# DeltaNet attention with an FNet block: loads 6 and 7 in program order on all engines, the second weight matrix ahead of the third inversion, GpSimd's arithmetic on VectorE, unread products ahead of load 0

## The chip, the cores and the metric

The kernel runs on one core of a Trainium2 chip. The time is the device time of one execution in microseconds (us); the figure for a kernel is the median of its runs. A profiled execution also has a span, from its first to its last instruction, and the mean clock that TensorE was granted (1.0 is full speed). The engines are called as the profile calls them: PE (TensorE, matmul; PEld is its loading of weights), DVE (VectorE), ACT (ScalarE), POOL (GpSimd) and SP (SyncE, which here only issues DMAs).

## What is computed

Attention of the "delta" kind, for B = 4 batches, H = 8 heads, S = 768 steps and heads of D = 48, then a block that mixes with Fourier transforms:

```python
k_n = k / (norm(k, axis=-1) + 1e-6)
for t in range(S):                       # one 48 x 48 state for each batch and head
    y[t]  = q[t] @ state
    state = state + beta[t] * outer(k_n[t], v[t] - k_n[t] @ state)
x  = y as (B, 768, 384)
u  = x + real(fft(fft(x, axis=1), axis=2))
un = (u - mean(u)) / sqrt(var(u) + 1e-6)
out = u + relu(un @ w_ch1) @ w_ch2       # w_ch1 384 x 1536, w_ch2 1536 x 384
```

All arrays are float32 but the two weight matrices, which arrive as float64 and are converted on the chip.

## The kernel before, in words

**Loads, rounds, batches.** The sequence is cut into 24 *loads*, g = 0 to 23: 128 steps of all 8 heads of one batch, 6 loads (`NL`) for a batch. A load has two chunks of 64 steps. Within a chunk the recurrence is solved with the inverse of a unit lower triangular matrix; between chunks the state goes on. Four loads (`RL`) make a *round*: their 32 triangular matrices are inverted together, all on DVE. Rounds 0 to 2 invert blocks of 16 (`invert16`, L451; the first transpose is L468, the row-by-row pairs are L510 and L513, the last transposes L516 and L518), rounds 3 to 5 blocks of 32 (`invert`, L392; transpose L398, pairs L439 and L443, last transposes L446 and L447). So the third inversion is `invert16(2)` and the fourth `invert(3)`. The matrix M that each fills is set to zero first, on POOL. In the four loads of the next round, the inverse is what everything else hangs on.

**The parts of a load.**
- *Keys* (`pre_a`, L316): the key rows are turned by four 128x128 transposes on PE (`turn`, L308; PE line L113), ACT copies them out as KT (L314), PE forms the products of keys with keys, and the triangular part goes to G and GU. In `gram16` (L351) ACT and DVE fill G (L372, L376, L378), and GU is made by DVE in one masked product for the first four loads (L383), by ACT in three small copies for the others (L388).
- *Queries* (`pre_q`, L524): the same turn gives QT; then products of keys and queries, masked by DVE into LQ (L548).
- *After the inversion* (`pre_m16`, L591, for rounds up to 2; `pre_m`, L551, later): the blocks of the inverse are put together to MT with ACT copies (Z L601, MT L617 and L640) and PE products, and V is scaled (L622 on DVE for loads under 8; on POOL otherwise, there and at L562). In batch 0 U0 and WT are made in addition.
- *Recurrence* (`step`, L671): `S,KT` products on PE, V minus these on DVE (L691), `V,MT` products, U copied out by ACT (L701), `U,K` products, and the new S on DVE (L730, L732).
- *Outputs* (`outputs`, L735): `S,QT` products into one PSUM pair, copied to x by ACT (L755), `U,LQ` products, added to x by DVE (L765). Chunk 0 of a batch's first load has no state, so its half of the pair is set to zero by DVE (L745) ahead of the products.

**After a batch's six loads** come `folds` (L772: sums and differences of rows and columns, L786 to L804; the two E of rows, L786 and L788, on POOL from batch 1 on, except in the last tile), `fourier` (L809: products with tables, x L873 to L876, statistics, the reciprocal root on POOL) and `mlp` (L889: un on DVE, turned by PE (`ptr`) and copied by ACT (L911, unT), the products `ph` with the first matrix, ReLU on ACT (L921, hT), the products `po` with the second matrix, the add to x L932, and the store). `mlp` of one batch is cut into pieces that are woven into the loads of the next batch.

**The weights** (`weights`, L221) are converted in 24 pieces of 384x128 or 128x384, 12 for each matrix. A piece arrives as two 32-bit words for each number. ACT converts the low word (L277) and a clamp (L272); DVE picks bits with five instructions (L278, L282, L283, L292, L294); POOL multiplies the two parts (L287), into w1 or w2; then SP issues the load of a later piece into the slot of the ring that came free. The ring has 4 slots for w1 and 3 for w2. Each `yield` is half a piece. The variable `conv` is this generator.

**What sets the order.** The parts are Python generators, and `advance` runs one of them to its next `yield`. Under `tc.manual_schedule(engines=...)` the named engines keep the order in which the program issues; the others are ordered by the framework's scheduler. Batch 0 is written out by hand, under PE, DVE, ACT and POOL. From load 6 on, `period(g, side)` (L991) does one load in six slots: the two chunks of the recurrence, the outputs, the next load's `pre_q` and `pre_m`, the keys and the inversion of the next round at so many yields for each slot, the folds, and `side`, the `mlp` of the batch before, up to a quota `want`. Loads 6 and 7 run under PE alone, loads 8 to 23 under all four:

```python
        inv = invert16(2)
    with tc.manual_schedule(engines={mybir.EngineType.PE}):
        drain(nq)
        for g in range(NL, NL + 2):
            period(g, side)
    with tc.manual_schedule(engines=engines):
```

DMAs are issued from SP, in program order unless the scheduler orders them, and a few from POOL and ACT at the start.

**Unread products.** Ahead of load 0's recurrence PE runs five products of 128x384 that nobody reads (`spin(5)`, L1122; the product is L1119), of `ident`, a part of the constant `pack`, with zeros. They come just before the first use of the first inverse.

All products pass one helper line each: L110 for products, L113 for transposes.

Of the kernel before, what the change touches and what calls it, by code (L numbers as in the profile page):

```python
# [20 lines left out]
RL = 4  # L21
RING = 7
V16 = 16
R16 = 3
# [40 lines left out]
def kernel(  # L65
# [126 lines left out]

    early = w2.rearrange("p c m -> p (c m)").rearrange("p (n h d) -> p n h d", h=8, d=64)
    nc.vector.memset(early[:, :, :, D:64], 0.0)
    early = [early[:, i] for i in range(9)]
# [25 lines left out]
    def weights():  # L221
# [13 lines left out]
        for last, pieces in enumerate(sets):  # L235
# [33 lines left out]
            for i in range(len(pieces) + 1):  # L269
                if i > 0:  # L270
                    lo0, hi0, man0, num0 = of(i - 1)
                    nc.scalar.activation(num0, num0, ACT.Relu, bias=low_e)  # L272
                if i < len(pieces):
                    lo, hi, man, num = of(i)


                    nc.scalar.activation(man, lo.bitcast(U32), ACT.Copy, scale=2.0 ** -52, bias=1.0)  # L277
                    nc.vector.tensor_scalar(num, hi, 0xFFFFF, None, op0=ALU.bitwise_and)  # L278
                yield
                if i > 0:  # L280

                    nc.vector.tensor_scalar(num0, num0, 255, 2.0 ** 23, op0=ALU.min, op1=ALU.mult)  # L282
                    nc.vector.scalar_tensor_tensor(num0, hi0, -2 ** 31, num0, op0=ALU.bitwise_and,  # L283
                                                   op1=ALU.bitwise_or)
                    dst = pieces[i - 1][1]
                    c = dst.shape[1]
                    nc.gpsimd.tensor_tensor(dst, man0.rearrange("p (c f) -> p c f", c=c),  # L287
                                            num0.bitcast(F32).rearrange("p (c f) -> p c f", c=c),
                                            op=ALU.mult)
                    stage(i - 1 + deep)  # L290
                if i < len(pieces):
                    nc.vector.scalar_tensor_tensor(man, num, 2.0 ** -20, man, op0=ALU.mult,  # L292
                                                   op1=ALU.add)
                    nc.vector.tensor_scalar(num, hi, 20, 0x7FF, op0=ALU.logical_shift_right,  # L294
                                            op1=ALU.bitwise_and)
                yield
# [54 lines left out]
    def gram16(g, KT, G):  # L351
# [3 lines left out]
        if g == 0:  # L355
            GXs["O"] = wk.tile([128, RL, 8, C], F32, tag="O", name="GU4")
        if first:
            GU = GXs["O"][:, g]
        else:
            GU = wk.tile([128, 8, C], F32, tag="GX", bufs=4, name="GU")  # L360
            nc.gpsimd.memset(GU[:, :, 0:V16], 0.0)
        GXs[g, 16] = GU
# [10 lines left out]
        for hh in range(2):  # L373
# [3 lines left out]
            else:  # L377
                nc.scalar.activation(dst[rw], src[rw, :, :, W:C], ACT.Copy)  # L378
        if g == 2 * RL - 1:
            yield  # L380
        dst = GU.rearrange("p (i a) s -> p a i s", a=2)
        if first:
            nc.vector.tensor_tensor(dst, src, m_up[:, None, None, :].broadcast_to([128, 2, 4, C]),  # L383
                                    op=ALU.mult)
        else:
            for e in range(1, 4):
                cs = slice(V16 * e, V16 * e + V16)
                nc.scalar.activation(dst[:, :, :, cs], src[:, :, :, cs], ACT.Copy,  # L388
                                     scale=m_ahead[:, e - 1:e])
        yield  # L390

    def invert(r):  # L392
# [3 lines left out]
        M = wk.tile([128, W, W], F32, tag="M", name="M")  # L396
        nc.gpsimd.memset(M, 0.0)
        nc.vector.transpose(A, G.rearrange("p m s -> p s m"))  # L398
# [52 lines left out]
    def invert16(r):  # L451
# [14 lines left out]
        A, M, Ad, Md = whole(A2), whole(M2), blocks(A2), blocks(M2)  # L466
        nc.gpsimd.memset(M2, 0.0)
        nc.vector.transpose(A, G.rearrange("p m s -> p s m"))  # L468
# [82 lines left out]
    def pre_m(g):  # L551
# [9 lines left out]
                                op=ALU.mult)  # L561
        nc.gpsimd.tensor_tensor(V.rearrange("p c j d -> p (c j) d"),  # L562
                                V.rearrange("p c j d -> p (c j) d"),
# [27 lines left out]
    def pre_m16(g):  # L591
# [28 lines left out]
        def scaled_v():  # L620
            V = Vs.pop(g)
            (nc.vector if g < 2 * RL else nc.gpsimd).tensor_tensor(  # L622
                V.rearrange("p c j d -> p (c j) d"), V.rearrange("p c j d -> p (c j) d"),
                nT[:, m8, None].broadcast_to([128, 8, D]), op=ALU.mult)
            return V
# [109 lines left out]
    def outputs(g):  # L735
# [7 lines left out]
        pq = ps_pair()  # L743
        if n == 0:
            nc.vector.memset(pq[full[0], :, 0:4 * D], 0.0)  # L745
        for j in range(2):
            for hh in range(2):
                for cc in range(2):
                    for jp in range(2):
                        if n == 0 and cc == 0:  # L750
# [3 lines left out]
                           S[(b, 2 * n + cc)][lo[jp], hh, j, :], j == 0 and hh == 0)  # L754
        nc.scalar.activation(x.rearrange("p (i a e) -> p a i e", a=2, e=D),  # L755
                             pq[:, :, 0:4 * D].rearrange("p a (i e) -> p a i e", e=D), ACT.Copy)
        yield
# [6 lines left out]
        xv = x.rearrange("p (h e) -> p h e", h=2)  # L764
        nc.vector.tensor_tensor(xv, xv, pl[:, :, 0:4 * D], op=ALU.add)  # L765
        yield
# [5 lines left out]
    def folds(b):  # L772
# [11 lines left out]
        for t in range(TH):  # L784
            eng = nc.gpsimd if b and t < TH - 1 else nc.vector
            eng.tensor_tensor(E[:, 0, t], x[:, t], x[:, TH + t], op=ALU.add)  # L786
            yield
            eng.tensor_tensor(E[:, 1, t], x[:, t], x[:, TH + t], op=ALU.subtract)  # L788
            yield
# [198 lines left out]
    done = 0  # L988
    pm = inv = late = None

    def period(g, side):  # L991


        nonlocal pm, inv, late, done, fold
        b, n = divmod(g, NL)
# [19 lines left out]
        if more:  # L1015
# [7 lines left out]
            elif g + 1 >= 2 * RL:  # L1023
                pm = pre_m16(g + 1)
                if not fresh:
                    behind[0].append(pm)
                for i in range(4):
                    pieces[i + (2 if fresh else 1)].append(pm)
        if not last_round and r > 1:
            if li == 0:  # L1030
                load_beta(r + 1)
            keys = {0: ((0, 1), (2, 3), (4, 5)), 1: ((0, 1),)}.get(li, ())
            for i, (s0, s1) in enumerate(keys):
                k4 = pre_a(RL * (r + 1) + 3 * li + i)
                behind[s0].append(k4)
                pieces[s1].append(k4)
        for i in range(SLOTS):
            if i == (2 if r + 1 < R16 else 3) and fresh and inv:
                drain(inv)
# [3 lines left out]
            if i == 5 and n + 1 == NL:  # L1043
                o = outputs(g)
                drain(o)
                late = None
            if li == 1 and i == 1 and r > 1 and not last_round:
                inv = invert(r + 1)
            if g == NL:
                advance(inv, 4)  # L1050
                advance(conv, 3)
            elif inv:
                advance(inv, 8 if r + 1 < R16 else 6)
            if n + 2 >= NL and 0 < i < 5:
# [7 lines left out]
            else:  # L1062

                want = 2 + KF + (2 + 2 * KF) * at // (2 * SLOTS)
                if n > 1:
                    want = 4 + 3 * KF + (PIECES - KEEP - 4 - 3 * KF) * (at - 2 * SLOTS) // (
                        SLOTS * (NL - 2))
            for p in behind[i]:
                advance(p)
            advance(side, want - done)  # L1070
            done = max(want, done)
        load_v(g + 2)

    engines = {mybir.EngineType.PE, mybir.EngineType.DVE, mybir.EngineType.Activation,
               mybir.EngineType.Pool}
    with tc.manual_schedule(engines=engines):
# [5 lines left out]
        ms = [pre_m16(g) for g in range(2 * RL)]  # L1082
        for g in range(RL):
            advance(keys[g])
            if g > 0:
                drain(keys[g - 1])
        drain(keys[RL - 1])
        advance(inv0, 2)
        for g in range(3):
# [21 lines left out]
        advance(keys[-1])  # L1111
        idle = wk.tile([128, DM], F32, tag="un", bufs=2, name="idle")
        nc.gpsimd.memset(idle, 0.0)
        unread = ps_post([128, 512], "unread")

        def spin(n):

            for _ in range(n):
                nc.tensor.matmul(unread[:, 0:DM], lhsT=ident, rhs=idle, start=True, stop=True,  # L1119
                                 skip_group_check=True)  # L1120

        spin(5)  # L1122

        advance(ms[0], 2)
        advance(qs[1])
# [10 lines left out]
        advance(inv1, 5)  # L1136
        drain(keys[-1])
        first = part(conv, 2 * KF + 2)
# [125 lines left out]
        for fc in range(KF):  # L1264
            if converted < 2 * KF + 2:
                convert(2)
            else:
                advance(conv)
            advance(side)
            if fc % 3 == 1:  # L1270
                advance(f)
# [8 lines left out]
        inv = invert16(2)  # L1280
    with tc.manual_schedule(engines={mybir.EngineType.PE}):
        drain(nq)
        for g in range(NL, NL + 2):
            period(g, side)
    with tc.manual_schedule(engines=engines):
        for b in range(1, B):
            for g in range(max(NL * b, NL + 2), NL * (b + 1)):
                period(g, side)
# [44 lines left out]
```

## Time and profile before

| | |
|---|---|
| runs | 762.54, 759.20 and 761.86 us, median 761.86 |
| the profiled execution's own time | 760.74 us |
| its span | 759.0 us |
| its mean granted clock | 0.973 |
| PE busy | 691.9 us, 91% of the span |
| DVE busy | 392.1 us, 52% |
| ACT busy | 246.7 us, 33% |
| POOL busy | 99.2 us, 13% |
| largest groups on PE | ph 207.8 us (864 products), po 204.7 us (576) |
| the chain that ended last | 74% PE, 19% DVE, 3% ACT, 3% issue, 1% DMA |

Where things lie in that execution: the keys of loads 0 to 3 up to 16 us, the first inversion 16.57 to 35.2, the second 39.2 to 77.2, the recurrence of batch 0 from 36 to 114, its Fourier part and the first pieces of its `mlp` to 164, loads 6 and 7 from 164 to 250 with the third inversion from 175.26 to 214.1, the fourth inversion 256.72 to 302.57. The pieces of w1 are converted from 80 us on, those of w2 up to 211.

How to read it: an entry `busy, mean ns | idle before, releaser` gives the time in which the rows of a group ran and the idle time of the engine just before them, with what ended it. In a time line the columns are start, duration, engine, line, operation, tile out and tiles in, shape, count, and in brackets the idle time ahead and its releaser. In the table of stretches the columns follow the names PE, PEld, DVE, ACT, POOL, then the granted clock, the share of DMA time and GB/s. In the slices each digit is a tenth of a fortieth of the span, 19 us.

### The profile page before, as it was taken

How to read it: one execution, taken by the hardware profiler on the slowest of the kernel's cores; microseconds unless marked ns; L12 is line 12 of the kernel's file. 1: busy time of each engine (PE TensorE's matmuls, PEld its weight loads, DVE VectorE, ACT ScalarE, POOL GpSimd, SP SyncE). 2: the span in 40 equal slices, each digit the busy share in tenths (PEclk: the TensorE clock that was granted, in tenths of full speed). 3: DMA queues.
4: the chain of work that ended last, by engine and by line, in shares of the span. 5: the costliest groups of instructions: out<-in, count | busy, mean ns of one | idle time of the engine just before them, and what ended most of it. 6: DMA issues, size and time to landing. Idle time of an engine off the chain costs nothing.

```text
span 759.0 us, 23046 instructions
## 1 busy us (share of the span) xinstructions
PE 691.9 (91%) x10162; PEld 534.2 (70%) x10162; DVE 392.1 (52%) x961; ACT 246.7 (33%) x610; POOL 99.2 (13%) x138
## 2 busy tenths in 40 slices
PE   5877779697899986999999999999999999999998
PEld 4666668586667655877867768877667678777684
DVE  4966896879942499343298228178512240600000
ACT  3533662566424311223422333233223221211120
POOL 7000120322300012001110220020100110100000
PEclk9999987798999999999999999999999999999999
DMA  9832353025212312002212221011120000000000
GB/s 151 215 67 43 78 136 92 24 58 133 74 32 55 67 34 44 12 11 48 54 41 49 44 44 29 1 31 24 43 44 12 13 12 0 22 1 21 11 11 22
DMA packets 111863, 36.10 MB, mean 48 GB/s; under 512 B 101873, under 2 KB 109842, under 8 KB 111762
## 3 DMA queue, kind: packets, MB, share of 16 engines
q1 hardware_dynamic: 109938, 33.86, 20.3%
q8 instruction: 80, 1.31, 0.7%
q0 software_dynamic: 640, 0.43, 0.4%
q10 hardware_dynamic: 1184, 0.33, 0.3%
q14 instruction: 21, 0.17, 0.1%
HBM read 29.88 MB, written 4.72 MB: 46 GB/s over the span
## 4 chain that ended last, share of the span: by engine, by line
PE 74%; DVE 19%; ACT 3%; issue 3%; DMA 1%; DVEq 0%; ACTq 0%
PE po L110 24%; PE ph L110 21%; PE one L110 14%; PE pair L110 9%; PE one L113 2%; DVE M L443 2%; DVE tmp L439 2%; PE ptr L113 1%; DVE wtmp L294 1%; DVE wtmp L283 1%; PE unread L1119 1%; DMA C<-in_k_dram 1%; DVE M L513 1%; DVE wtmp L292 1%; PE pf L110 1%
## 5 line engine op out<-in xcount | busy, mean ns | idle before, releaser
L110 PE MATMUL ph<-unT,w 128*128 128x256 f32 x864 | 207.8, 392 | 0.7 <-ACT unT L911 0.7
L110 PE MATMUL po<-w,hT 128*128 128x384 f32 x576 | 204.7, 495 | 0.0
L110 PEld LDWEIGHTS ph<-unT,w 128*128 128x128 f32 x864 | 162.7, 194 | 25.5 <-issue 1.0
L110 PEld LDWEIGHTS po<-w,hT 128*128 128x128 f32 x576 | 103.5, 190 | 56.4
L921 ACT ACTIVATE hT<-ph 128x256 f32<-128x256 f32 x144 | 54.9, 382 | 148.5 <-PE ph L110 148.4
L932 DVE TENSOR_TENSOR x<-x,po 128x384 f32<-128x384 f32 x24 | 13.2, 550 | 107.0 <-PE po L110 107.0
L732 DVE TENSOR_TENSOR S<-S,pair 128x192 f32<-128x192 f32 x40 | 13.9, 348 | 73.4 <-PE pair L110 73.4
L110 PEld LDWEIGHTS one<-V,MT 64*64 64x64 f32 x768 | 29.5, 138 | 19.7 <-issue 8.9
L873 DVE TENSOR_TENSOR x<-x,one 128x193 f32<-128x193 f32 x24 | 8.5, 353 | 64.8 <-ACT Q L864 64.8
L110 PE MATMUL one<-V,MT 64*64 64x48 f32 x768 | 34.8, 225 | 3.8 <-DVE V L691 1.8
L443 DVE TENSOR_TENSOR M<-M,tmp 128x31 f32<-128x31 f32 (+15 forms) x93 | 35.1, 378 | 3.2
L439 DVE TENSOR_TENSOR tmp<-A,M 128x31 f32<-128x31 f32 (+15 forms) x93 | 33.5, 360 | 2.4
L110 PE MATMUL one<-MT,ND 64*64 64x64 f32 x768 | 29.1, 226 | 1.8 <-ACT MT L640 0.7
L691 DVE TENSOR_TENSOR V<-V,pair 128x192 f32<-128x192 f32 x33 | 11.5, 349 | 36.9 <-PE pair L110 33.2
L559 POOL TENSOR_TENSOR MT<-A,pack 128x512 f32<-128x512 f32 x12 | 12.8, 1065 | 131.1 <-PE one L110 64.4
L110 PEld LDWEIGHTS one<-dtab,F 97*128 97x128 f32 (+1 forms) x192 | 25.7, 193 | 5.3 <-ACT F L868 0.5
L110 PEld LDWEIGHTS one<-MT,ND 64*64 64x64 f32 x768 | 26.5, 141 | 2.9 <-issue 1.1
L314 ACT ACTIVATE QT<-one 128x512 f32<-128x512 f32 x24 | 14.3, 596 | 42.1 <-PE one L113 42.1
L287 POOL TENSOR_TENSOR w<-wtmp 128x384 f32<-128x384 f32 x12 | 14.6, 1217 | 89.7 <-DVE wtmp L283 89.7
L110 PE MATMUL pair<-KT 48*32 48x64 f32 (+1 forms) x1152 | 22.7, 247 | 4.0 <-ACT KT L314 3.9
L110 PEld LDWEIGHTS pair<-U,K 64*64 64x64 f32 x704 | 15.5, 135 | 15.3 <-issue 12.4
L110 PE MATMUL one<-dtab,F 97*128 97x97 f32 (+1 forms) x192 | 26.2, 277 | 0.0
(173 smaller groups left out, 1009.5 us busy)
## 6 DMA issues: line engine op xcount, KB each, us to landing
w<-in_moe_w_ch_dram SPq DMA_DIRECT2D x12, 384.0 KB
E<-in_moe_w_ch_dram SPq DMA_DIRECT2D x12, 384.0 KB
out_dram<-x SPq DMA_DIRECT2D x24, 192.0 KB
K<-in_k_dram SPq DMA_DIRECT2D x92, 48.0 KB
V<-in_v_dram SPq DMA_DIRECT2D x92, 48.0 KB
C<-in_k_dram SPq DMA_DIRECT2D x18, 192.0 KB
Q<-in_q_dram SPq DMA_DIRECT2D x18, 192.0 KB
w<-in_q_dram SPq DMA_DIRECT2D x6, 192.0 KB
```

What stands on the lines that cost most here:

```text
L110: nc.tensor.matmul(o, lhsT=lhsT, rhs=rhs, start=start, stop=stop, skip_group_check=True)
L113: nc.tensor.matmul(o, lhsT=src, rhs=ident[0:src.shape[0], 0:src.shape[0]], is_transpose=True, start=start, stop=True, skip_group_check=True)
L287: nc.gpsimd.tensor_tensor(dst, man0.rearrange("p (c f) -> p c f", c=c), num0.bitcast(F32).rearrange("p (c f) -> p c f", c=c), op=ALU.mult)
L314: nc.scalar.activation(dst.rearrange("p h j t -> p (h j t)"), pt, ACT.Copy)
L439: nc.vector.tensor_tensor(t, A[:, j + 1:W, j:j + 1].broadcast_to([128, n, j + 1]), M[:, j:j + 1, 0:j + 1].broadcast_to([128, n, j + 1]), o ...
L443: nc.vector.tensor_tensor(M[:, j + 1:W, 0:j + 1], M[:, j + 1:W, 0:j + 1], t, op=ALU.add)
L559: nc.gpsimd.tensor_tensor(MT, MTd[:, m8, None, :].broadcast_to([128, 8, 2, W]), m_blk[:, None, :, None].broadcast_to([128, 8, 2, W]), op=A ...
L691: nc.vector.tensor_tensor(R4, R4, pw[:, :, 0:2 * D].rearrange("p a (j e) -> p a j e", e=D), op=ALU.subtract)
L732: nc.vector.tensor_tensor(s1v, s0.rearrange("p h j e -> p h (j e)"), pk, op=ALU.add)
L873: nc.vector.tensor_tensor(near, near, pb[:, 0, 0:MH + 1], op=ALU.add)
L921: nc.scalar.activation(hT[:, fc, :], ph, ACT.Relu)
L932: nc.vector.tensor_tensor(x[:, T, :], x[:, T, :], po, op=ALU.add)
```

## The change

**The start.** The zeros `idle` are made at the very top by DVE. Three unread products (`spin(3)`, now of `idle` with itself) run ahead of load 0's transposes, and `spin(6)` stands where `spin(5)` stood. The keys of loads 0 to 3 are advanced in another order, with one more yield in `gram16`: the turn of load 1 comes before load 0's grams, and so on; the GU of loads 2 and 3 is made by ACT copies, with their zeros set by POOL, and those of 0 and 1 by DVE as before.

**GpSimd's arithmetic on VectorE.** The weights' product (L287), the zeros of GU, the zeros of M (but for the first inversion's), the scaling of V, and the folds' E of rows go from POOL to DVE. POOL keeps the product of MT with its mask in `pre_m`, the reciprocal root, zeros at the start, and its DMA issues.

**Outputs of a batch's first load.** The zeros of L745 go. ACT copies only the upper half of the pair, DVE adds only there, and the lower half of x is copied by ACT straight from the second pair.

**Loads 6 and 7** run under all four engines in program order. In load 6 the conversion of w2 is advanced three times in each of the slots 0 to 3 and then drained; the third inversion takes no yields there and four in each of load 6's slots 4 and 5 (before, four in each of the six). Elsewhere an inversion takes 6 for each slot up to round 2 and 5 later, where it was 8 or 6. At the end of load 7 the inversion is drained and the next `pre_m16` runs in four steps with a piece of `side` after each. In the first `mlp` stretch `conv` is advanced once more for each of the last groups.

**Later rounds.** An inversion from round 3 on starts in slot 0 instead of 1, and is drained in slot 3. The last key of a round is advanced one slot earlier, at the end of the load before. The quota for `side` is 14 at the batch's start and then 13, 12, 6, 5, 5 and 5 pieces for the six loads.

```diff
+    idle = wk.tile([128, DM], F32, tag="un", bufs=2, name="idle")
+    nc.vector.memset(idle, 0.0)
...
-                    nc.gpsimd.tensor_tensor(dst, man0.rearrange("p (c f) -> p c f", c=c),
+                    nc.vector.tensor_tensor(dst, man0.rearrange("p (c f) -> p c f", c=c),
...
-        if first:
+        if g < 2:
             nc.vector.tensor_tensor(dst, src, m_up[:, None, None, :].broadcast_to([128, 2, 4, C]),
                                     op=ALU.mult)
...
-        nc.gpsimd.memset(M2, 0.0)
+        (nc.vector if r else nc.gpsimd).memset(M2, 0.0)
...
-            (nc.vector if g < 2 * RL else nc.gpsimd).tensor_tensor(
+            nc.vector.tensor_tensor(
...
-        if n == 0:
-            nc.vector.memset(pq[full[0], :, 0:4 * D], 0.0)
...
+        rw = full[1] if n == 0 else slice(0, 128)
+        nc.scalar.activation(x[rw].rearrange("p (i a e) -> p a i e", a=2, e=D),
+                             pq[rw, :, 0:4 * D].rearrange("p a (i e) -> p a i e", e=D), ACT.Copy)
...
+        nc.vector.tensor_tensor(xv[rw], xv[rw], pl[rw, :, 0:4 * D], op=ALU.add)
+        if n == 0:
+            nc.scalar.activation(xv[full[0]], pl[full[0], :, 0:4 * D], ACT.Copy)
...
-            eng = nc.gpsimd if b and t < TH - 1 else nc.vector
...
-                for i in range(4):
-                    pieces[i + (2 if fresh else 1)].append(pm)
+                for i in range(0 if fresh else 4):
+                    pieces[i + 1].append(pm)
...
-            if g == NL:
-                advance(inv, 4)
-                advance(conv, 3)
+            if g == NL and i < 4:
+                advance(conv)
             elif inv:
-                advance(inv, 8 if r + 1 < R16 else 6)
+                advance(inv, 4 if g == NL else 6 if r < R16 else 5)
...
             for p in behind[i]:
                 advance(p)
+            if g == NL and i < 4:
+                advance(conv)
             advance(side, want - done)
             done = max(want, done)
+            if g == NL and i < 4:
+                advance(conv)
+                if i == 3:
+                    drain(conv)
         load_v(g + 2)
+        if g == 2 * RL - 1:
+
+            drain(inv)
+            inv = None
+            for _ in range(4):
+                advance(pm)
+                advance(side)
+                done += 1
...
+        spin(3)
+        for i in (0, 1, 0, 2, 0, 1, 3, 1, 2, 3):
+            advance(keys[i])
...
-        spin(5)
+        spin(6)
...
+            if fc > 7:
+                advance(conv)
...
-    with tc.manual_schedule(engines={mybir.EngineType.PE}):
         drain(nq)
-        for g in range(NL, NL + 2):
-            period(g, side)
-    with tc.manual_schedule(engines=engines):
         for b in range(1, B):
-            for g in range(max(NL * b, NL + 2), NL * (b + 1)):
+            for g in range(NL * b, NL * (b + 1)):
                 period(g, side)
```

## The prediction

> **What bounds the kernel now.** I read the page first (busy shares, slices), then the stretches of 19 us, then the time line of each engine, and the rows of TensorE with an idle time in front of them.
>
> ```profile
> PE 691.9 (91%) x10162; PEld 534.2 (70%) x10162; DVE 392.1 (52%) x961; ACT 246.7 (33%) x610; POOL 99.2 (13%) x138
> PE   5877779697899986999999999999999999999998
> DVE  4966896879942499343298228178512240600000
> PEclk9999987798999999999999999999999999999999
> ```
>
> TensorE (PE) is the bound, and nearly without gaps from slice 16 on (304 us). What can be won lies before that: there PE has gaps, the granted clock is 0.7 to 0.9 in places, and VectorE (DVE) is at 8 or 9 tenths instead. The stretches, columns PE, PEld, DVE, ACT, POOL busy, clock, DMA share, GB/s:
>
> ```profile
> 171.00:190.00 19.00, 14.35 (x182) 11.93 (x172) 19.00 (x50) 11.27 (x27) 5.36 (x7) 0.82 0.50 132
> 190.00:209.00 19.00, 15.71 (x162) 12.23 (x160) 18.09 (x51) 7.68 (x18) 6.32 (x6) 0.91 0.29 71
> 285.00:304.00 19.00, 13.17 (x273) 10.49 (x266) 18.07 (x42) 3.72 (x10) 3.83 (x4) 1.00 0.20 44
> ```
>
> In all three DVE is full and PE waits. Whom PE waits for stands in brackets:
>
> ```profile
> 62.80 0.49 PE L110 MATMUL pair<-S,QT 48*64 48x48 f32 x10 [1.91 <-DVE pair L745]
> 176.55 1.13 PE L110 MATMUL pair<-QT,KT 48*64 48x64 f32 x32 [4.65 <-ACT QT L314]
> 194.85 0.83 PE L110 MATMUL pair<-S,QT 48*64 48x48 f32 x16 [3.29 <-DVE pair L745]
> 302.83 0.45 PE L110 MATMUL pair<-S,KT 48*64 48x48 f32 x16 [3.56 <-DVE S L732]
> 522.75 0.67 PE L110 MATMUL pair<-S,QT 48*64 48x48 f32 x16 [1.50 <-DVE pair L745]
> ```
>
> And what GpSimd (POOL) does to DVE:
>
> ```profile
> 80.92 0.36 DVE L294 TENSOR_SCALAR wtmp<-w 128x384 int32<-128x384 int32 x1
> 84.77 1.24 POOL L287 TENSOR_TENSOR w<-wtmp 128x384 f32<-128x384 f32 x1 [48.49 <-DVE wtmp L283]
> 85.19 1.04 DVE L294 TENSOR_SCALAR wtmp<-w 128x384 int32<-128x384 int32 x1
> ```
>
> The same L294 takes 0.36 alone and 1.04 beside the POOL product: it ends when POOL does. 12 of the 24 L294 are long in this way, and where L294 isn't, another DVE row of that moment is (L480 1.01 instead of 0.22, L499 1.44 instead of 0.69).
>
> All sums stand against the profiled execution's own 760.74 us (span 759.0). The median of the runs is 761.86, 1.1 above it; I add that at the end. A difference of 0.5% (3.8 us) is about what a measurement of this kernel tells from none.
>
> **Part 1, the start (0 to 36 us).** Inversion 0 begins with the transpose L468 at 16.57, behind two products L383 of 0.69 on DVE. Two of the four move to ScalarE (ACT) as six small copies (L388: 0.29 each, 1.76 in all), which ACT does while DVE transposes for 1.89: L468 starts about 1.0 earlier. What is late next is PE: five unread products run from 29.47 for 6.11, and the first product of load 0 stands behind them at 35.50, though its input was ready at 34.31. The change has six: cold, 7.3, from 28.5 to 35.8; if the clock comes up 5.3 us after their start, as it did, 35.1. So the 1.0 is eaten (-0.4 to +0.3). The three unread products ahead of load 0 take 3.7 from about 1.4 on (a memset of 0.4 first), and end at 5.1, 0.3 after the place of load 0's transposes (4.81); the next ones wait for their load until 6.62 anyway. Do they bring the clock up? These rows bear on it:
>
> ```profile
> 14.14 1.11 PE L113 MATMUL one<-pack,Q 128*128 128x128 f32 x4
> 29.47 6.11 PE L1119 MATMUL unread<-idle,pack 128*128 128x384 f32 x10
> 36.58 0.66 PE L113 MATMUL one<-pack,w 128*128 128x128 f32 x4
> ```
>
> Four transposes take 1.11 after seven us of unbroken PE work, and 0.66 after the unread products. If PE stayed fast from 5 us to 36, the six would take 3.9 and load 0 start when its input is there, 33.3: -2.2. That is the other bound. I take -0.5, near the row at 14.14, as PE idles from 16.1 to 19.3 in between. [...]
>
> **Part 2, batch 0 (36 to 114).** The memset L745 goes: PE waited 1.91 for it, DVE's next S could come 1.5 earlier (63.75 to 62.28). Next late is ACT: the other half of x is now a copy of 0.47 on ACT behind two rows of 0.60 and 0.90, and frees the bank that the row at 65.82 wants: -0.6. Bounds -1.5 and -0.6, I take -0.9. Of seven weight pieces from 84 to 112 each leaves 0.69 of blocking and brings a product on DVE of 0.55 (L622, same shape): 7 x -0.14 = -1.0, and one small memset comes (0.2). DVE is 3.9 of 4 busy there, so this counts. M's memset (1.0 as L194) comes to DVE ahead of inversion 1 and lies in the 1.98 that DVE idles before 43.12; without that cover it costs 1.0. Sum **-1.7**. From 114 to 164 nothing: DVE has idle time ahead of L873 each time (2.6, 2.4, 1.5).
>
> **Part 3, loads 6 and 7 (164 to 250).** DVE's work from 173 to 214: blocking that goes, 6.7 (ten long rows against their short ones); what comes, nine products of 0.55, V 0.55, M's memset 1.0, a small one 0.2; the pair memset goes, 0.4. Net -0.3. Order is the unknown: DVE, ACT and POOL followed a scheduler here and now follow the program. Bound below: PE's waits of 3.29 and 0.7 go, and the clock of 0.50 (176 to 180) and 0.67 (196 to 200) comes back for 2: -6. Bound above: PE waited 4.65 because QT stood on ACT behind a weight row that waited for its load. Two more half pieces are now ahead of QT. DVE has 4.5 of weight rows more to do before it, less 1.5 of blocking, plus 0.3 of memsets, and ACT's chain from there is 3.5: QT at 180 instead of 176.5. After it DVE does seven pieces of about 3.0 (2.56 of work, and 0.4 of waiting for ACT as at 145.11) in order, and load 6's V sits behind five of them: PE waits there 3 to 4. The third inversion then begins after the last piece and ends about 8 later; its first reader stands behind 14 more products on w2 and the recurrence of load 7, 11 later on PE. Together +5. I take **-0.5**, from the row with DVE at 19.00 of 19.00: a full engine's stretch goes with its work.
>
> **Part 4, the fourth inversion (250 to 304).** DVE does it from 256.72 to 302.57, 45.85. Blocking of 3.3 goes (L443 at 1.06 instead of 0.36 and so on), two V and two E of 0.5 come: 44.6. It starts earlier: the last key's products move from behind V,MT and Z,GU to right behind U,LQ, which ends about 1.0 after the S,KT at 250.20: transpose at 252.5. So it ends at 297.1, and the S,KT of 302.83 comes at 297.5: -5.3. Two groups of ph (1.47 each) leave the stretch and are done later, where PE is full: +2.9. The clock of 0.57 from 304 to 308 costs 1.7; I count half. Sum **-3.2**, bounds -4.1 and 0.
>
> **Part 5, the rest.** The wait at 522.75 goes, that of 0.82 at 538.65 may (DVE's rate per slot is 5 instead of 6): **-1.5**, bounds -2.3 and 0. Twelve E and eleven V of 0.55 come to DVE, which is idle two thirds of that time; nothing else moves PE.
>
> **Sum.** -0.5 - 1.7 - 0.5 - 3.2 - 1.5 = -7.4: 753.3 for the profiled execution, 754.4 beside the median.
>
> **Rivals.** (a) *The order of loads 6 and 7 costs what it saves*: part 3 at +5, 759.9. For it: three engines in one order, with QT and V behind weight rows. Against: DVE has no idle time to lose but what the order makes. (b) *The same place, slower*: the weight load closes a ring. Piece 8's load stands on SP behind the load of a Q tile, which waits for PE's transposes, which wait for QT on ACT, which waits for a piece's load. A load takes 4.2 from its release (169.3) to its reader (173.49). Three exposed loads cost 12.6 instead of the -0.5: 767.5. It decides from 10.7 on, at the third exposed load. For it: the 1.30 that ACT waited at 173.49. Against: three slots in the ring. (c) *The order is right and the early clock holds*: part 3 at -6, part 1 at -2.2: 747.2. (d) The products ahead of load 0 don't do what they are put there for: load 0's transposes stay near 1.1; that is 754.9, inside the forecast.
>
> **Chances.** Forecast 0.50 (0.03 of it within 0.5%), (a) 0.24 (0.03 of it faster), (b) 0.12, (c) 0.14. Faster 0.47 + 0.03 + 0.14 = 0.64; same 0.03 + 0.21 = 0.24; slower 0.12. The range runs from 745, below (c), to 763, above (a) with the small bounds; (b) is left out, 0.12, and the rest of the 0.2 are sums beyond both.
>
> **What would show it.** No L294 near 1.04 any more; no wait of S,QT for a memset; the 128x128 transposes at 5 to 16 us at 1.1 (if 0.66, part 1 was too small); QT's reader on PE after a wait of 4 to 9 around 176; the transpose L401 some 4 ahead of 256.7 less what came before; the wait for S at the end of that inversion down to under 3.5. Wrong would be: a wait of PE over 5 at load 6's V, or cold stretches that move to places where PE is dense.

## The result, and the profile after

The changed kernel takes **787.27 us** (median of 4 runs, 780.54 to 787.70) against 761.65: ratio 1.0321, 95% interval 1.0261 to 1.0381. It is 25.6 us slower. The profiled execution took 787.45, with a span of 785.7 and a mean granted clock of 0.941 instead of 0.973. In the changed kernel the lines stand 2 to 4 further down: QT and KT are L316, the clamp of a weight piece L274, hT L925, the last transposes of `invert` L449 and L450.

The page, with the lines that answer to those shown of before:

```profile
PE 704.5 (90%) x10170; PEld 540.8 (69%) x10170; DVE 403.9 (51%) x1021; ACT 249.6 (32%) x620; POOL 39.5 (5%) x73
PE   7886877857889897999999899999899999999998
DVE  6877987686662389533277437358621322600000
PEclk8799967897999899999999899999899999999999
```

POOL's 60 us are gone and VectorE is no fuller as a share. PE, nearly without gaps from 304 us on before, now has a slice under 9 at 440 us and one at 560, and the clock dips there too. The stretches of 19 us around loads 6 and 7 and the fourth inversion (columns as before):

```profile
171.00:190.00 19.00, 10.25 (x118) 8.02 (x122) 13.47 (x34) 8.80 (x23) 1.23 (x2) 0.64 0.34 95
190.00:209.00 19.00, 14.20 (x158) 11.51 (x152) 14.42 (x32) 6.96 (x18) 0.00 (x0) 0.95 0.21 53
285.00:304.00 19.00, 14.85 (x326) 10.61 (x326) 17.97 (x46) 4.53 (x10) 0.00 (x0) 1.00 0.16 32
```

VectorE, full at 19.00 in the first one before, is busy for only 13.47 there, and PE for 10.25 instead of 14.35, at 0.64 of the clock. So no engine is full: they wait for each other. PE's rows with a long wait, on its time line:

```profile
171.97 0.69 PE L110 MATMUL pair<-KT 48*64 48x64 f32 x32 [3.17 <-ACT KT L316]
179.33 0.92 PE L110 MATMUL pair<-QT,KT 48*64 48x64 f32 x24 [5.94 <-ACT QT L316]
205.82 5.84 PE L110 MATMUL ph<-unT,w 128*128 128x256 f32 x18 [3.47 <-ACT hT L925]
233.60 1.32 PE L110 MATMUL one<-Z,GU 64*64 64x64 f32 x32 [2.04 <-ACT Z L604]
269.63 1.97 PE L110 MATMUL one<-Z,GU 64*64 64x64 f32 x32 [2.97 <-ACT Z L604]
317.39 0.45 PE L110 MATMUL pair<-S,KT 48*64 48x48 f32 x16 [0.77 <-DVE S L735]
440.21 1.06 PE L110 MATMUL one<-G,GX 32*32 32x32 f32 x32 [2.81 <-DVE G L450]
563.18 1.06 PE L110 MATMUL one<-G,GX 32*32 32x32 f32 x32 [3.23 <-DVE G L450]
```

The waits for the zeroing are gone, and that for S (317.39, before 302.83) fell from 3.56 to 0.77. In their place stand waits for ACT in loads 6 and 7, and from 440 on waits for G, the inverse itself.

To find where the time went, I set equal points of PE's work beside each other: the same products of the same load in both traces. The changed kernel is 4.4 us ahead at the first S,WT (44.11 against 48.52) and 5.6 ahead at 118; 3.6 ahead at load 10's keys (161.03 against 164.59); then 1.4 *behind* at load 11's (171.97), 5.8 at load 6's first S,KT (193.49), 13.4 at load 9's first (263.61), 17.6 at its second (278.10), 14.6 at the end of the fourth inversion (317.39). Then come 5.5 at 440 us and 5.9 at 563, some 2.6 are won at 522 to 540, and 3.4 go in steps of 1 or less from 317 to 487 (1.7 of them at two waits of 1.24 and 0.91 for QT, at 391.92 and 479.65): 26.7 behind at the end. The large losses are few, and each lies at one of the waits above.

And the last three are larger than their waits: 2.81 of wait cost 5.5, 3.23 cost 5.9, 2.97 cost some 6 (4.2 between load 9's two S,KT, and 1.8 of products that stood in this stretch before and now stand elsewhere). The row at 440.21 shows why: the G,GX products took 1.06, and 0.69 elsewhere. PE ran at half clock from 439.2 to 446.1. In all, the record of the clock has 92 us at half speed, against 41 before. But the record begins at 5.7 us here and only at 34.8 before, and the profile's mean counts the time ahead of it as full speed, though the rows there take as long as at half clock (before, four transposes take 1.1, as here at 17.17 and 19.28 within a recorded stretch at half, and not 0.66; here the three unread products take 1.40 each, and 0.71 at 442.69 in `e15_filled4`). With that time counted as half the figures are 98 and 76: 22 us more at half clock, worth at most 11 of the 25.6 (an estimate: half of PE's work in that time). PE's idle time, span less busy, is 14.1 more (81.2 against 67.1).

### The profile page after: what moved, and what is told of

Its sections match the earlier page's. It is cut to its first block, busy times and chain, and to the rows that moved or that the text cites. A ratio compares the mean times of both kernels' runs of the same rounds, so it can differ in the third digit from the quotient of the medians.

```text
span 785.7 us, 22935 instructions
## 1 busy us (share of the span) xinstructions
PE 704.5 (90%) x10170; PEld 540.8 (69%) x10170; DVE 403.9 (51%) x1021; ACT 249.6 (32%) x620; POOL 39.5 (5%) x73
## 4 chain that ended last, share of the span: by engine, by line
PE 74%; DVE 18%; ACT 5%; issue 2%; DMA 0%; DVEq 0%; ACTq 0%
PE po L110 23%; PE ph L110 22%; PE one L110 14%; PE pair L110 9%; PE one L113 2%; DVE tmp L442 2%; DVE M L446 1%; PE unread L1109 1%; PE ptr L113 1%; DVE w L289 1%; DVE G L450 1%; DVE A L401 1%; PE pf L110 1%; ACT O L274 1%; DVE Z L641 1%
## 5 line engine op out<-in xcount | busy, mean ns | idle before, releaser
L110 PE MATMUL po<-w,hT 128*128 128x384 f32 x576 | 208.6, 502 | 0.0
L925 ACT ACTIVATE hT<-ph 128x256 f32<-128x256 f32 x144 | 54.9, 383 | 152.7 <-PE ph L110 152.6
L446 DVE TENSOR_TENSOR M<-M,tmp 128x31 f32<-128x31 f32 (+15 forms) x93 | 32.7, 352 | 2.8
L110 PE MATMUL pair<-KT 48*32 48x64 f32 (+1 forms) x1152 | 20.9, 237 | 8.2 <-ACT KT L316 6.6
L110 PE MATMUL one<-Z,GU 64*64 64x64 f32 x384 | 16.5, 245 | 11.5 <-ACT Z L604 10.9
L110 PEld LDWEIGHTS pair<-KT 48*32 48x32 f32 (+1 forms) x1152 | 17.3, 127 | 12.4 <-ACT KT L316 8.0
```

The source lines that it names most:

```text
L110: nc.tensor.matmul(o, lhsT=lhsT, rhs=rhs, start=start, stop=stop, skip_group_check=True)
L446: nc.vector.tensor_tensor(M[:, j + 1:W, 0:j + 1], M[:, j + 1:W, 0:j + 1], t, op=ALU.add)
L925: nc.scalar.activation(hT[:, fc, :], ph, ACT.Relu)
```

## The experiments

Theory A: the start's lead is real, and the time is lost to new waits of PE that the new orders make, each with a fall of the clock behind it. Rival C: VectorE, with GpSimd's arithmetic on top, is too full. Later theories narrow A down. The kernel before ran beside each (medians 761.95 to 762.92); differences from the changed kernel are against 787.27.

**1. What each half of the change does.** `e1_start`: on the kernel before, the new start alone.

```diff
+        spin(3)
+        for i in (0, 1, 0, 2, 0, 1, 3, 1, 2, 3):
+            advance(keys[i])
...
-        spin(5)
+        spin(6)
```

> The kernel before with the new start alone (zeros made first, three unread products ahead of load 0's transposes, the new order of the keys, GU of loads 2 and 3 by ACT, six unread products instead of five). Theory A (the start's lead is real and is lost later, to waits that other parts make): the first S,WT stands 4.4 us earlier, as in the changed kernel (44.11 instead of 48.52), and the end too: 757. Rival B (the lead is eaten by the next wait on a load or on ACT): 761 to 762, no difference.

Measured: 762.11, ratio 0.9973 (0.9951 to 0.9996). At 45 us PE is 2.9 ahead, but the lead is gone at 87, and no wait took it. Both kernels wait alike there, and only in one does the clock fall (first fence the kernel before, second `e1_start`; time lines of PE):

```profile
76.47 1.15 PE L110 MATMUL one<-Z,GU 64*64 64x64 f32 x32 [2.48 <-ACT Z L601]
```
```profile
73.67 1.98 PE L110 MATMUL one<-Z,GU 64*64 64x64 f32 x32 [2.53 <-ACT Z L604]
```

The same products, 1.15 and 1.98; the mean clock is 1.00 from 75 to 91 us in the one and 0.57 from 72 to 88 in the other. So B by the time, but by the clock, not by a next wait.

`e4_pool`: on the kernel before, GpSimd's arithmetic on VectorE alone.

> The kernel before with only GpSimd's arithmetic moved to VectorE. Theory A: the blocking of VectorE goes (12 rows of 1.04 that become 0.36) and 0.55 a product comes, so 758 to 762. Rival C: VectorE, full from 171 to 209 us and from 266 to 304, becomes the bound there: 765 or more.

Measured: 759.26, ratio 0.9972 (0.9949 to 0.9994). A holds: VectorE is not too full for it. C falls.

`e2_rounds_back`: the changed kernel with the later inversions as before.

```diff
-            if li == 1 and i == 0 and r > 1 and not last_round:
+            if li == 1 and i == 1 and r > 1 and not last_round:
...
-                advance(inv, 4 if g == NL else 6 if r < R16 else 5)
+                advance(inv, 4 if g == NL else 6)
```

> The changed kernel with the inversions of rounds 3 on as before: start in slot 1, six yields a slot, the last key in its old slot. Theory A (the lost time is PE's new waits, each followed by some 7 us at half clock: 2.97 at 269.63 with 6.6 lost, 2.81 at 440.21 with 5.5, 3.23 at 563.18 with 5.9): these three go, the waits for S at the end of the inversion come back for about 3 to 5, so 787 - 18 + 4 = 773. Rival C (VectorE has taken on GpSimd's arithmetic and is late for that reason): the waits stay, 783 to 787.

Measured: 775.33, so 12 us come back. A holds.

`e3_loads_back`: the changed kernel with loads 6 and 7 as before (the `manual_schedule` of PE alone, conversion and inversion side by side, no `if fc > 7` steps).

> The changed kernel with loads 6 and 7 as before: only PE in program order, the third inversion and the second weight side by side, no extra conversion steps in the first MLP stretch. Theory A: what was lost from 161 to 245 us comes back (4.9 at load 6's keys, 4.5 at its queries, 5.5 at the end of load 7, less 0.5 gained between them): 787 - 14 = 773. Rival C (VectorE is too full there with the weights' products): less than half of it comes back, 780 or more.

Measured: 767.80, so 19.5 us come back, more than A had.

`e5_three`: on the kernel before, start, arithmetic and outputs together.

> The kernel before with three parts of the change and nothing else: the new start, GpSimd's arithmetic on VectorE, and the outputs without the zeroed half. If the parts add up: start -0.7 (median against median), arithmetic -3.6, outputs -2 (PE's waits of 1.9, 3.3 and 1.5 for the zeroing go, something else is late next): 756 to 757, against 762.8. If the start's lead is kept once VectorE is no longer blocked (theory A): 753. If the lead is taken by the clock and not by a wait (rival D): 757 or more.

Measured: **754.75**, ratio 0.9906 (0.9871 to 0.9941). These three win 7.2; start and arithmetic alone won 0.7 and 3.6, so some 2.9 is left for the outputs (which were not run alone) and for what the parts give each other. The sum closes: -7.2 + 19.5 + 12 = 24.3, against 25.6.

**2. Loads 6 and 7: the order, or the new places?**

`e8_pe_only`: the changed program, where loads 6 and 7 are in program order on PE alone.

```diff
+    with tc.manual_schedule(engines={mybir.EngineType.PE}):
+        for g in range(NL, NL + 2):
+            period(g, side)
```

> The changed kernel, with the second weight ahead of the third inversion and the extra steps, but loads 6 and 7 in program order on PE alone, the other engines ordered by the scheduler. Theory F (program order costs): most of the 19.5 us that the kernel with loads 6 and 7 as before wins comes back, 770. Theory G (the new place of the conversion and of the inversion costs): 783 to 787.

Measured: 773.21. F: 14 of the 19.5 are program order, and 5.4 are left for the new places. `e7_vector_order` comes from the other side: loads 6 and 7 as before, with VectorE in order too (the same with ACT in order as well was not run).

> The changed kernel with loads 6 and 7 advanced as before (conversion and inversion side by side), but with VectorE in program order there as well as PE; ACT and GpSimd are left to the scheduler. It stands against the kernel with loads 6 and 7 wholly as before, 767.8. Theory F (program order in itself costs, since a row that waits for a load holds up the rows behind it): 773 or more. Theory G (the order is all right, what costs is the new place of the conversion and the third inversion): 766 to 770.

Measured: 779.27, 11.5 slower than without it: F again. PE waits there 3.96, 2.27 and 2.39 for S and V, which stand behind weight rows.

`e13_act_free` and `e14_vector_free`: the changed kernel with one engine each left to the scheduler in these loads.

> The changed kernel with ACT alone left to the scheduler in loads 6 and 7; PE, VectorE and GpSimd keep program order. Theory M (what costs in program order is ACT's: hT, unT, QT and x stand there behind the clamp of a weight piece that waits for VectorE, and behind the square root of the third inversion): most of the 14 us between this kernel and the one with PE alone in order (773.2) comes back: 774 to 777. Rival N (it is VectorE's order, where V and S stand behind weight rows): 784 or more.

> The changed kernel with VectorE alone left to the scheduler in loads 6 and 7; PE, ACT and GpSimd keep program order. Theory M (ACT's order costs): 783 or more. Rival N (VectorE's order costs): 774 to 777. If each of the two kernels wins about half, both orders cost, each by its own waits.

Measured: 781.91 and 780.28, 5.4 and 7.0 less than 787.27. Neither M nor N alone: both orders cost. The medians are less apart than their runs are spread (777 to 788), so the traces have to say it: from load 11's keys to load 9's first S,KT the changed kernel takes 91.6, and these two are 5.4 and 8.5 shorter, which together is about what `e8_pe_only`, with all but PE freed, has (13.4). In ACT's list of waits from 160 to 245 us (in total, times, longest) the changed kernel has

```profile
ACT O L274 <- DVE O L296: 15.9, 8, 3.6
...
ACT nrm L477 <- DVE A L471: 2.8, 1, 2.8
```

and `e8_pe_only`, with the same work, has

```profile
ACT O L274 <- DVE O L296: 8.6, 5, 3.6
```

A clamp L274 waits for VectorE's piece, and hT, unT or QT stand behind it. The square root is the clearest case, on ACT's time line of the changed kernel:

```profile
205.11 0.26 ACT L477 ACTIVATE nrm<-A 128x32 f32<-128x32 f32 x1 [2.83 <-DVE A L471]
205.39 0.66 ACT L925 ACTIVATE hT<-ph 128x256 f32<-128x256 f32 x2
```

Two groups of ph are ready for their hT, ACT waits 2.83 for the transpose of the third inversion, and PE waits 3.47 for hT (205.82).

`e6_no_extra`: the changed kernel without the two lines `if fc > 7: advance(conv)`.

> The changed kernel without the extra conversion step for the last four groups of the first MLP stretch; load 6 has four half pieces more to do. Theory A (the two extra pieces stand on ACT ahead of load 11's keys and of hT, and PE waits 1.41 and 3.17 for them, then loses the clock): the loss of 4.9 at 172 us goes, of which up to 2 comes back in load 6: 783 to 785. Rival E (the pieces cost the same wherever they stand, since VectorE and ACT are the bound until the weights are done): 787.

Measured: 785.58. In its trace load 10's keys stand at the same time (161.07 against 161.03) and QT's products start 8.4 earlier (170.90 against 179.33), as A had it, but 6.8 of that is lost again by load 7's first S,KT (209.98 against 211.59), at waits of 5.17 for U and 4.19 for hT that the changed kernel has not or has shorter. So A had the waits right and E the outcome; a median that is 1.7 lower doesn't tell the two apart. That the conversion must end before the third inversion begins, wherever its pieces stand, would explain it, but no run shows it.

**3. The later inversions.** `e9_rate`: six yields instead of five in rounds 4 and 5.

> The changed kernel with the inversions of rounds 4 and 5 at six yields a slot instead of five; nothing else is undone. Theory H (the lower rate alone ends these inversions too late for the next load's products): PE's waits of 2.81 and 3.23 for G, the inverse, go, with the 2.7 and 2.6 that the clock takes after them: 787 - 11 = 776. Rival I (the inversions end late because the loads behind them come late, or because VectorE has the folds' and V's products now): the waits stay, 785 to 788.

Measured: 780.17, 7.1 less. In the trace the two waits are gone and the points after them are 5.5 and 5.9 earlier: H by the trace; the profiled run had lost 3.4 to the clock by the end of batch 0, where the two programs are the same, and the median shows the lesser gain.

`e10_inv_behind`: the start of the inversion behind the slot's queries.

```diff
             for p in behind[i]:
                 advance(p)
+            if li == 1 and i == 0 and r > 1 and not last_round:
+                inv = invert(r + 1)
+                advance(inv, 6 if r < R16 else 5)
```

> The changed kernel with the inversions from round 3 on still begun in slot 0, but issued behind that slot's queries and ACT copies instead of ahead of them. Theory J (ACT's square root of the inversion waits for VectorE's zeroing and transpose, and QT and Z stand behind it): the wait of 2.97 at 269.63 and its loss of 6.6 go, those of 1.24 and 0.91 for QT too: 779 to 781. Rival (Z is late for another reason): 785 to 788.

Measured: 783.78, 3.5 less; its runs lie from 779.46 to 786.60. In its trace the wait of 2.97 is gone, and PE gains 4.6 between load 9's first S,KT and load 10's first (a wait of 0.88 for Z is left); the two waits for QT are gone too. J by the trace, with a smaller size by the median. The row of the square root says it, in ACT's time line of the changed kernel:

```profile
268.05 0.26 ACT L408 ACTIVATE nrm<-A 128x32 f32<-128x32 f32 x1 [1.87 <-DVE A L401]
268.21 0.58 ACT L316 ACTIVATE QT<-one 128x512 f32<-128x512 f32 x1
268.69 0.89 ACT L604 ACTIVATE Z<-G,pack 128x256 f32<-128x256 f32 x2
```

VectorE pays as well: in program order it then stands idle for 3.85 behind PE's late U,K, in the middle of the inversion (its time line, changed kernel):

```profile
275.16 0.35 DVE L735 TENSOR_TENSOR S<-S,pair 128x192 f32<-128x192 f32 x1 [3.85 <-PE pair L110]
```

From its first transpose to the end of its last the inversion takes 49.98 in the changed kernel, 45.34 in `e10_inv_behind` and 45.85 before.

**4. The wait or the clock?** `e11_filled`: the changed kernel, with unread products in front of the reader of G.

```diff
+                if p is pm and i == 3 and fresh and r > 1:
+                    unread3 = ps_one()
+                    for _ in range(8):
+                        mm(unread3[:, 0:DM], ident, w1[:, 0, 0:DM], True)
```

> The changed kernel with eight unread products of 128x384 on PE just where it waits 2.81 and 3.23 for the inverse (the last load of rounds 3 and 4); nothing is taken away, PE only has something to do in these waits. Theory K (half of what such a wait costs is the clock that falls to half for some 7 us after it): the two stretches of 6.8 us at half clock go, 787 - 5 = 782. Rival L (a wait costs its own length): 787 or a little more.

Measured: 793.00. The total falls outside both: `r > 1` holds for round 2 as well, where PE did not wait (5.4 lost), and eight products take 5.43, not 2.8. At the two places themselves K shows: from S,KT to S,KT it is 14.19 instead of 14.31 at 440, though PE does 2.6 more there. So `e15_filled4`, four products, rounds 3 and 4 only (`r > 2`, `range(4)`):

> The changed kernel with four unread products of 128x384 on PE (0.68 us each by the run with eight, 2.7 in all) just where it waits 2.81 and 3.23 for the inverse, in rounds 3 and 4 alone. Theory K (half of what such a wait costs is the clock at half speed after it): 11.3 of loss become 6, so 787 - 5 = 782, though no wait goes. Rival L (a wait costs its own length only): 787.

Measured: 783.84, 3.4 less, within the spread of both kernels' runs (780 to 788). The profiled run, at 787.81, had lost 4.8 in batch 0, where the programs are the same; each of the two places itself is 2.5 shorter in it, 5.0 in all (the 440 us place, time line of PE):

```profile
442.31 0.45 PE L110 MATMUL pair<-S,KT 48*64 48x48 f32 x16
442.69 2.85 PE L110 MATMUL one<-w,pack 128*128 128x384 f32 x8
445.65 0.69 PE L110 MATMUL one<-G,GX 32*32 32x32 f32 x32
...
454.10 0.45 PE L110 MATMUL pair<-S,KT 48*64 48x48 f32 x16
```

G,GX starts 3.34 after S,KT, as late as without them (3.26 there), but takes 0.69 and not 1.06, and the next S,KT comes after 11.79 instead of 14.31. K holds at these two places: a wait of 2.8 costs 2.8 and another 2.5 of clock.

**5. The version that the runs point to.** `e12_best`: `e5_three` with the last key one slot earlier, and the inversions of rounds 3 to 5 begun in slot 0 behind its queries at six yields; loads 6 and 7 as before.

> The kernel with the three good parts (754.75), and in addition the last key one slot earlier and the inversions of rounds 3 to 5 begun in slot 0, behind that slot's queries, at six yields a slot. If the earlier start shortens VectorE's stretch as the prediction had it: the waits for S of 2.75 and 3.14 fall under 1 and the clock stays: 750 to 752. If something else is late there: 754 to 756.

Measured: **750.05**, ratio 0.9835 (0.9811 to 0.9859): faster than both kernels, and where the first expectation had it. Of the waits for S the second fell under 1 (0.96, from 3.14 in `e5_three`), the first only to 2.30, but the clock stays after both.

## Why the prediction was wrong

The forecast was 754.4 (745 to 763); 787.27 lies above the slower rival too. Point by point:

- **Part 1** (-0.5, bounds -2.2 and +0.3): too small in the trace. The lead at the first S,WT was 4.4 (2.9 with the start alone). The transposes took 0.66 instead of 1.1 (the row it named as the sign): the clock came up at 5.7 us, at the end of the three unread products, and stayed to 12.6, so the inversion's transpose began at 13.38, 3.2 earlier and not 1.0. Then the clock fell for 17 us, as the prediction had feared, but ahead of the gap that it named: since 5.7 PE had waited only 0.41 and 0.90, and the one of 2.74 came at 13.4. Its price of a cold unread product, 1.22, is the mean of a row that ended at full clock; three cold ones took 4.21, 1.40 each. By medians the part alone was worth 0.7, since what the clock does later is not fixed.
- **Part 2** (-1.7): near. From 44 to 118 us PE won 1.2 more, in spite of a new wait of 2.89 for S (103.76).
- **Part 3** (-0.5, bounds -6 and +5): this is the step that failed. "A full engine's stretch goes with its work" took VectorE's 19.00 of 19.00 for a bound; the change made it 13.47, and loads 6 and 7 cost 19.5. The upper bound priced two waits, at QT and at V. That at QT came (180 forecast, 179.33 measured; the place is partly luck, since PE came 3.6 early to load 10's keys and lost 3.17 and 1.41 at waits for KT and hT that the prediction did not have), that at V did not. What it left out: ACT's order (hT and unT behind a clamp), the square root of the third inversion ahead of hT, and the fall of the clock behind new waits. The end of the third inversion it took for covered by PE's other work; PE waited 2.04 for Z there. Program order is 14 of the 19.5, the new places 5.4. (By its own terms VectorE's work is 0.4 less, not 0.3.)
- **Part 4** (-3.2): VectorE began the fourth inversion 2.6 after load 9's first S,KT, near the forecast's 2.3, but starting one slot earlier set the square root ahead of QT and Z: 2.97 of wait, some 6 of loss, and an inversion of 49.98 instead of 44.6. The wait for S fell to 0.77 because PE itself came late, not because the inversion ended sooner. With the start behind the queries it takes 45.34 (`e10_inv_behind`) and 45.49 (`e12_best`), so the forecast was near for VectorE alone. The prediction followed the earlier start on VectorE and not the one ACT row that goes with it.
- **Part 5** (-1.5): both waits that it named went (some 2.6). But it read the lower rate only as room for S. The inversions of rounds 4 and 5 then end in the slot where their reader stands: two waits for G, 11.4 in the trace.
- **GpSimd's share** came as forecast: all 24 rows of L294 (now L296) take 0.36, and the part alone won 3.6.
- **Rival (a)** had the mechanism, QT behind weight rows in one order, and its sign (a wait of 5.94 at QT), at a quarter of the size. **Rival (b)** had the direction and a wrong mechanism: no exposed load. ACT's waits from 160 to 245 us in the changed kernel list none for a weight's load.
- **The clock** stands in the sums only as a gain: in the centre once, at 304 us and by half, and in the better bounds. It was about half of what the three waits of 2.81, 2.97 and 3.23 cost (5.5, some 6 and 5.9). What the prediction named as a sign of being wrong, cold stretches where PE is dense, came at 439 and 562 us.

In the changed kernel the clock fell within waits of 2.97, 2.81 and 3.23 (at 268.56, 439.23 and 562.11) and 0.8 behind one of 2.04 (at 234.43); at waits of 2.5 it fell in one run and not in another (73.67 and 76.47 above). In the clock records of both kernels every stretch at half speed that ends within the span lasts 3.41, 6.83, 10.24, 13.65 or 17.07 us. How long a wait has to be for the clock to fall, no run shows. That the gap from 16.1 to 19.3 (3.19) would cost the clock was the author's estimate, and not shown: in the kernel before, four transposes take 1.11 ahead of it (14.14) and behind it (20.35).

What stays open: which rows make up the 5.4 of the new places, the outputs' own share, and why the clock stayed at half from 16 to 29.6 us, with PE at work.

## What to carry to other kernels

When an engine is put into program order, look for each of its rows that waits for another engine, and for what stands behind that row: here a cheap row (a square root of 0.26) ahead of a copy that PE wants cost some 6 us, more than the 3.2 that part 4 was to save. Price a new wait of PE by those here: 2.81, 2.97 and 3.23 us cost their length plus 2.5 to 3 for the clock. Waits of 2.5 for Z cost the clock in the changed kernel (70.76), in `e1_start` (73.67) and in `e8_pe_only` (70.64), where the row behind takes 1.97 or 1.98, and not in the kernel before (76.47), where it takes 1.15. If the wait cannot be removed, try unread products in it: in `e15_filled4` they gave the second part back, 2.5 at each of the two places. And a slower rate for a background chain has to be checked against its end, not only against what it competes with.

## What the runs showed of the hardware

The same program's time varies: the changed kernel took 780.54 to 787.70. Profiled runs that are the same program to there, and within 0.1 us of each other at 66 us, differ by up to 4.1 us at the last S,WT of batch 0 (112.50 in the changed kernel, 116.60 in `e2_rounds_back`). Both wait 2.5 just ahead of 70.8 us, and the clock falls there for 3.41 in the one and for 13.65 in the other. Why, no run shows. A part worth under 4 us in batch 0 is therefore seen in one trace and not in another, and only medians, or points of equal work with the clock beside them, tell it.
